# Last pair of an attention and soft-MoE kernel: 1 / sum applied behind the product with v, logits in three steps, 22 dummy transposes

## The chip, the cores and the metric

One core of a Trainium2 chip runs the whole kernel. The metric is the device time of one execution in microseconds (us); several executions are timed and their median is given. A profile of one more execution gives the span of its instructions, every instruction's start and duration, and the clock that was granted to TensorE.

The engines are PE (TensorE matmuls; PEld its weight loads), DVE (VectorE), ACT (ScalarE), POOL (GpSimd) and SP (SyncE, which issues all DMAs here). Each engine runs its instructions in the order of its queue; only semaphores tie the queues together.

## The reference

Batch 8, 8 heads, 576 tokens, head width 64, all in f32. With `tau` 0.02:

```python
scores = (q @ k.T) / 8
scores = where(scores >= max(scores, -1) - tau, scores, -1e9)
attn   = exp(scores - max(scores, -1))
attn   = attn / (sum(attn, -1) + 1e-9)
x      = concat over heads (attn @ v)             # 4608 tokens x 512
logits = x @ phi                                  # 32 slots, 4 for each of 8 experts
d = softmax(logits over all 4608 tokens);  slot_in = d.T @ x
slot_out[e] = relu(slot_in[e] @ w1[e]) @ w2[e]    # 512 -> 1024 -> 512
out = softmax(logits over the slots) @ slot_out
```

A softmax over all tokens stands between attention and the experts: no expert can start before the last token's logits are there.

## The kernel before, in words

**Attention.** The 64 (batch, head) problems are worked as 32 pairs of heads, four pairs to a batch. A pair has 576 queries x 2 heads, cut into nine chunks `i` of 128 rows: chunks 0 to 7 are four token blocks `c` for each head `h`, chunk 8 holds the 64 left-over tokens of both heads. For each chunk PE multiplies q and k (L554, L559), DVE copies the scores out negated with their row maximum (L566, "mx"), ACT takes the exponential (L576, "ex"), POOL makes the threshold (L579, "thr"), and DVE zeroes what lies under it and sums the rest (L582, "st"; the sum goes to `r[:, i]`). The probabilities lie in `p2` (one tile for each `c`) and `pL` (chunk 8). PE transposes them in 64x64 blocks (helper `ptr`, L481), ACT copies the transposes to `pTa` (c = 0, 1), `pTb` (c = 2, 3 and the left-over) and `pTl` (helper `act_copy`, L486, and L654), and PE multiplies with v in two products (L669): *a* of 256 tokens from `pTa`, *b* of 320 tokens from `pTb`. The result, features x tokens, is copied to `xT[j]`; it is transposed again (L481) into `x`, tokens x features.

**Where 1 / sum goes in.** In 31 pairs POOL scales `x` by 1 / sum behind the product (L684), and PE and ACT transpose that back into `xT` (L689, L692); only chunk 8 is scaled ahead (L613). In the last pair (`late`) the probabilities themselves are scaled as soon as a block's sums are there: two small DVE instructions make 1 / sum (L589, L591), and each chunk is multiplied with it (L595; POOL does seven chunks, DVE chunk 6; L600: ACT chunk 7). Then come the transposes.

**Dispatch.** Behind the four pairs of a batch, `dispatch(b)` transposes the left-over tokens of the four `xT` (`xl`), multiplies the four `xT` with phi (`logits`, L747, one group of 64 matmul records), takes the running maximum (L752, L755), its exponentials (L757, L759), and adds the batch's weighted tokens to `acc` (L794, L799, L807). In the last batch `scale` and `slot_in` (L719) turn `acc` into `siT`, the transposed slot inputs (L722, into the room of `phi_sb`).

**Experts.** 64 weight tiles of 512 KB are read (`load_unit`, L461 for w1, L463 for w2): 26 ahead of time into `w` tiles, 20 into `host` tiles that are laid over the attention's buffers as these come free (the pool of a `host` tile waits for the last use of the buffers below it), and 18 into `w` tiles behind the first layer's use of them. SP issues them in that order. `stage1` (L971) is the first layer, `stage2` (L1005) the second; the last quarter of stage2 writes `h00e` and `h11e`. `combine` writes the output.

**Order.** The attention part is not in program order. Each operation has a duration estimate and a rank (`nom`, from `TABLE`, added to the pair's base); a list planner (`Order.plan`) steps through time, and on each engine takes the ready operation of lowest rank for which buffers are free. So a rank decides only between operations that are ready together. PSUM has four regions, which QK scores, transposes and products share.

**Dummy transposes.** WARM transposes of the identity (L473, tile `ps`) depend on the last pair's last PE operation alone and have the highest rank: PE runs one whenever nothing else is ready, and what is left over is run at the end, ahead of stage1, in PE's queue.

Of the kernel before, what the change touches and what calls it, by code (L numbers as in the profile page):

```python
# [12 lines left out]
AF = mybir.ActivationFunctionType  # L13
ALU = mybir.AluOpType
# [16 lines left out]
REGIONS = 4  # L31
NPRE = 26
UP = 22
WARM = 38
LATE_DVE = (6,)
LATE_ACT = (7,)
FILL = 14
NHOST = 20
TABLE = {}
for _n, _v in (  # L40
# [8 lines left out]
    ]),  # L49
    ("last", [  # L50
# [7 lines left out]
    ]),  # L58
    ("end", [
        635.02, 222.30, 635.03, 884.35, 786.79, 194.11, 221.66, 209.51, 492.40, 213.82, 653.01, 233.76, 801.84, 524.02,  # L60
        811.00, 884.36, 248.25, 903.87, 542.06, 811.02, 658.66, 811.01, 811.01, 227.55, 666.83, 796.50, 632.21, 881.94,
        491.74, 653.02, 786.80,
    ]),
    ("soft", [
        27.63, 27.62, -312.54, 26.80, 28.26, -7.62,
    ]),
    ("batch", [
        -62.11, -152.03, -63.33, -1010.94, -1010.93, -130.22, -93.56, -111.14, -36.34, -160.31, -58.44, -111.55, -1032.75, -27.29,
# [6 lines left out]
        1608.61, 22.81, -920.27,  # L75
    ]),
    ("new2", [
        1255.54, -750.92, -123.71,
    ]),
    ("new3", [  # L80
        1682.14, -780.86, -618.82,
    ]),
# [39 lines left out]
           ae=0.5, x=6.0, xe=6.3, D=1.0)  # L122
# [218 lines left out]
def softmax_attention_soft_moe(  # L341
# [143 lines left out]
    def act_copy(n, nom, r, w, io):  # L485
        G.add("ACT", 51 + 0.833 * n, nom, lambda: nc.scalar.copy(*io()), r, w)  # L486

    def copy(on_dve, n, nom, r, w, io):
        if on_dve:
            G.add("DVE", 69 + 1.04 * n, nom, lambda: nc.vector.tensor_copy(*io()), r, w)  # L490
        else:
            act_copy(n, nom, r, w, io)

    def dve(dur, nom, r, w, fn):
        G.add("DVE", dur, nom, fn, r, w)

    batch = {}

    def batch_state(b):
# [6 lines left out]
    def pair(p):  # L506
# [10 lines left out]
        def pool(dur, nom, fn, r, w):  # L517
            G.add("POOL", dur, nom, fn, r, w)
# [27 lines left out]
        for i in range(N9):  # L546
# [37 lines left out]
                    scalar=thr.t, in1=view().rearrange("p (a k) -> p a k", a=2),  # L584
                    op0=ALU.is_le, op1=ALU.mult, accum_out=r.t[:, i:i + 1]))

            if late and (i == 8 or h == 1):
                e = slice(i // 2 * 2, i + 1)
                dve(68, t + OFF['ri'], [r[k] for k in range(i // 2 * 2, i + 1)], [ri[c]], lambda e=e: nc.vector.tensor_scalar(  # L589
                    out=ri.t[:, e], in0=r.t[:, e], scalar1=1e-9, scalar2=None, op0=ALU.add))  # L590
                dve(75, t + OFF['ri'], [], [ri[c]], lambda e=e: nc.vector.reciprocal(ri.t[:, e], ri.t[:, e]))  # L591
                for k in range(i // 2 * 2, i + 1):
                    dst_, view_ = (pL, lambda: pL.t) if i == 8 else (
                        p2s[c][k % 2], lambda c=c, k=k: p2s[c].t[:, k % 2 * S:(k % 2 + 1) * S])
                    f = lambda e, k=k, view=view_: e.tensor_scalar(  # L595
                        out=view(), in0=view(), scalar1=ri.t[:, k:k + 1], **one)
                    if k in LATE_DVE:
                        dve(740, t + OFF['sc'], [ri[c]], [dst_], lambda f=f: f(nc.vector))
                    elif k in LATE_ACT:
                        G.add("ACT", 650, t + OFF['sc'], lambda k=k, view=view_: nc.scalar.activation(  # L600
                            view(), view(), AF.Copy, scale=ri.t[:, k:k + 1]), [ri[c]], [dst_])
                    else:
                        pool(725, t + OFF['sc'], lambda f=f: f(nc.gpsimd), [ri[c]], [dst_])
            elif i == 8:
                e = slice(i // 2 * 2, i + 1)
                pool(292, t + OFF['ri'], lambda e=e: nc.gpsimd.tensor_scalar(
                    out=ri.t[:, e], in0=r.t[:, e], scalar1=1e-9, scalar2=1.0, op0=ALU.add, op1=ALU.mult),
                    [r[k] for k in range(e.start, e.stop)], [ri[c]])
                dve(84, t + OFF['ri'], [], [ri[c]], lambda e=e: nc.vector.reciprocal(ri.t[:, e], ri.t[:, e]))
                for k in range(e.start, e.stop):  # L610
                    dst_, view_ = (pL, lambda: pL.t) if i == 8 else (
                        p2s[c][k % 2], lambda c=c, k=k: p2s[c].t[:, k % 2 * S:(k % 2 + 1) * S])
                    pool(725, t + OFF['sc'], lambda k=k, view=view_: nc.gpsimd.tensor_scalar(  # L613
                        out=view(), in0=view(), scalar1=ri.t[:, k:k + 1], **one), [ri[c]], [dst_])
            elif not late and h == 1:
                if i == 7:
                    pool(292, t + OFF['ri'], lambda: nc.gpsimd.tensor_scalar(
                        out=ri.t[:, 0:8], in0=r.t[:, 0:8], scalar1=1e-9, scalar2=1.0, op0=ALU.add, op1=ALU.mult),
                        [r[k] for k in range(8)], [ri[0]])
                    dve(84, t + OFF['ri'], [], [ri[0]], lambda: nc.vector.reciprocal(ri.t[:, 0:8], ri.t[:, 0:8]))  # L620
                    G.skip(2)
                else:
                    G.skip(4)
# [19 lines left out]
            if i == 8:  # L643


                w = Buf("s")
                ptr(7, t + OFF['tt'], [p2s[2], p2s[3], pL], [w, pTb["t", 8], pTl["t", 8]], lambda w=w: [
                    (w.t, k * 64, [pL.t[rows[g], g * SL + k * 128:][:, 0:128] for g in range(2)]) for k in range(4)] + [
                    (w.t, 256, [pL.t[rows[0], S - 128:S], pL.t[rows[1], 0:128]])] + left_keys(2, 320, w))
                act_copy(256, t + OFF['te'], [w], [pTl[2]], lambda w=w: left_out(2, 320, w))  # L650
                act_copy(512, t + OFF['te'], [w], [pTb["L"]], lambda w=w: (
                    pTb.t[:, :, :, SM - QA:S - QA], w.t[:, :, 0:256].rearrange("p g (k q) -> p g k q", k=4)))
                for g in range(2):
                    G.add("ACT", 225, t + OFF['te'], lambda w=w, g=g: nc.scalar.copy(  # L654
                        pTl.t[rows[g], SM:S], w.t[rows[1 - g], g, 256:320]), [w], [pTl["L", g]])


        u = t0 + N9
        for a, (pT, q) in enumerate(((pTa, slice(0, QA)), (pTb, slice(QA, S)))):
            n0 = u + OFF['a1' if a else 'a0']  # L660
            w = bank_of(p == NP - 1)
            n = q.stop - q.start
            rl = [pTl[0]] if a == 0 else [pTl[2], pTl["L", 0], pTl["L", 1]]

            def mm(w=w, n=n, q=q, pT=pT):
                for kb in range(5):
                    for h in range(2):
                        v0, p0 = ((h * 4 + kb) * 64, pT.t[:, h, kb, :]) if kb < 4 else (SM + h * 64, pTl.t[:, q])
                        nc.tensor.matmul(  # L669
                            lone(w)[h * 64:(h + 1) * 64, 0:n], vv.t[:, v0:v0 + 64], p0,  # L670
                            start=(kb == 0), stop=(kb == 4), tile_position=(0, h * 64), skip_group_check=True)
            G.add("PE", 5 * (4 + 1.669 * n), n0, mm, [pT, vv] + rl, [w, xT["t"]], mode=COLS)
            copy(p == NP - 1 and a, n, n0 + OFF['ae'], [w], [xT[a]], lambda w=w, q=q, n=n: (xT.t[:, q], lone(w)[:, 0:n]))

        w = Buf("s")
        ptr(4, u + OFF['x'], [xT], [w, x["t", j]], lambda w=w: [
# [49 lines left out]
    def dispatch(b):  # L726
# [13 lines left out]

        wl = bank_of(b == B - 1)

        def logits():
            for o, q in ((slice(0, 128), lambda c: slice(c * 128, c * 128 + 128)), (slice(128, 192), lambda c: slice(SM, S))):
                for k in range(HP):
                    for c in range(4):
                        nc.tensor.matmul(  # L747
                            lone(wl)[c * 32:(c + 1) * 32, o], phi_sb[:, k, :], xT[k].t[:, q(c)], start=(k == 0),
                            stop=(k == HP - 1), tile_position=(0, 32 * c), skip_group_check=True)
        G.add("PE", 1313, u + 1, logits, xT + [ph], [wl], mode=COLS4)  # L750
        new = batch_state(b + 1)["M"]
        dve(269, u + 1.3, [wl], [M["own"]] if b else [new["run"]], lambda: nc.vector.tensor_reduce(  # L752
            out=M.t[:, 0:1] if b else new.t[:, 1:2], in_=lone(wl)[:, 0:192], axis=AX.X, op=ALU.max, negate=True))
# [392 lines left out]
```

## Time and profile before

| | |
|---|---|
| median of 3 runs (lowest, highest) | 554.12 us (554.01, 554.78) |
| profiled execution: time, span | 553.97 us, 552.2 us |
| granted TensorE clock, mean over the span | 0.988 of 2.4 GHz |
| busy share of the span | PE 96%, DVE 85%, ACT 83%, POOL 45% |
| read from HBM, written | 72.42 MB, 9.44 MB |

Attention fills the span to about 478 us, the last dispatch runs to 489 us, the experts to 520 us, and the combination and the writing of the output to the end. In the rows, "idle before" is the time in which the engine stood still ahead of the group, with what ended it; `x16` counts records, of which one f32 matmul makes two and a transpose one.

### The profile page before, as it was taken

The numbers are of one execution on the slowest core, as the hardware profiler recorded it, in microseconds if no ns is written. First come the engines' busy times: TensorE is split into PE (matmuls) and PEld (weight loads), VectorE is DVE, ScalarE is ACT, GpSimd is POOL, SyncE is SP. The second block draws the span as 40 slices with busy tenths as digits, with TensorE's granted clock in tenths as the row PEclk, the third lists the DMA queues.
The fourth block names the chain that finished last, engine by engine and source line by source line (L and its number), as shares of the span: only waits on it lengthen the run. The fifth ranks groups of instructions, "written<-read, shape, count | busy, mean of one in ns | idle before, by whom it ended". The sixth has DMA issues, their size and how long they took to land.

```text
span 552.2 us, 18305 instructions
## 1 busy us (share of the span) xinstructions
PE 530.8 (96%) x7022; PEld 340.9 (62%) x7022; DVE 470.6 (85%) x1326; ACT 458.6 (83%) x790; POOL 247.5 (45%) x478
## 2 busy tenths in 40 slices
PE   8999999999999999999999999999999998899991
PEld 6666666666666666666666666666666665654570
DVE  6999998999999998999999989998999999212192
ACT  3899998999999989998999899998999898511171
POOL 2554554554554453546454545554555547021030
PEclk9999999999999999999999999999999999899996
DMA  6355555555545543333133323333333523979498
GB/s 174 73 164 168 166 165 167 166 167 166 165 121 177 175 140 118 96 89 90 40 97 92 89 65 90 89 91 90 90 91 89 129 76 115 368 311 404 166 363 321
DMA packets 31990, 83.03 MB, mean 150 GB/s; under 512 B 4640, under 2 KB 12832, under 8 KB 31904
## 3 DMA queue, kind: packets, MB, share of 16 engines
q1 hardware_dynamic: 31904, 81.87, 48.4%
q8 instruction: 55, 0.90, 0.7%
q14 instruction: 31, 0.25, 0.2%
HBM read 72.42 MB, written 9.44 MB: 148 GB/s over the span
## 4 chain that ended last, share of the span: by engine, by line
PE 88%; DVE 4%; ACT 3%; issue 2%; POOL 1%; DVEq 0%; POOLq 0%; ACTq 0%
PE ps L669 29%; PE ps L554 24%; PE ps L481 17%; PE ps L559 3%; PE h L971 3%; PE so L1005 2%; PE ps L689 2%; PE ps L747 2%; PE ps L473 2%; PE ps L794 1%; DVE p L582 1%; PE up L421 1%; ACT pTa L486 1%; DVE ss L566 1%; DVE host L1057 1%
## 5 line engine op out<-in xcount | busy, mean ns | idle before, releaser
L566 DVE TENSOR_SCALAR_CACHE_REDUCE ss<-ps 128x576 f32<-128x576 f32 x288 | 208.9, 752 | 13.2 <-ACT pTl L486 4.9
L579 POOL TENSOR_SCALAR thr<-nmx,pabs 128x1 f32<-128x1 f32 x288 | 132.0, 460 | 179.2 <-DVE ss L566 159.6
L582 DVE SCALAR_TENSOR_TENSOR p<-ss,thr,p 128x576 f32<-128x576 f32 x256 | 202.7, 826 | 3.4 <-ACT p L576 3.1
L576 ACT ACTIVATE p<-ss,nmx 128x576 f32<-128x576 f32 x256 | 188.0, 778 | 18.8 <-DVE ss L566 18.7
L554 PE MATMUL ps<-k,q 64*128 64x288 f32 x1024 | 166.8, 427 | 0.9 <-ACT pTb L486 0.4
L481 PE MATMUL ps<-ident,p 64*128 64x64 f32 x2304 | 99.0, 225 | 3.5 <-ACT pTa L486 2.1
L481 PEld LDWEIGHTS ps<-ident,p 64*128 64x128 f32 x2304 | 88.4, 139 | 20.7 <-ACT pTa L486 3.8
L554 PEld LDWEIGHTS ps<-k,q 64*128 64x128 f32 x1024 | 83.3, 188 | 21.8 <-ACT pTl L654 5.8
L486 ACT COPY pTb<-ps 128x1024 f32<-128x1024 f32 (+1 forms) x96 | 83.7, 873 | 5.1 <-PE ps L481 2.9
L669 PE MATMUL ps<-pTb,vv 128*64 128x320 f32 x512 | 75.9, 438 | 0.0
L486 ACT COPY pTa<-ps 128x1024 f32<-128x1024 f32 x64 | 64.9, 1017 | 0.4 <-PE ps L481 0.4
L669 PE MATMUL ps<-pTa,vv 128*64 128x256 f32 x512 | 62.9, 388 | 0.0
L669 PEld LDWEIGHTS ps<-pTb,vv 128*64 128x64 f32 x512 | 33.9, 136 | 36.3 <-issue 8.5
L669 PEld LDWEIGHTS ps<-pTa,vv 128*64 128x64 f32 x512 | 34.2, 138 | 26.6 <-DVE ss L566 8.5
L669 PE MATMUL ps<-pTl,vv 128*64 128x256 f32 (+1 forms) x256 | 41.9, 406 | 0.0
L684 POOL TENSOR_TENSOR x<-x,ri 128x512 f32<-128x512 f32 x31 | 32.8, 1058 | 4.8 <-ACT x L486 4.8
L486 ACT COPY xT<-ps 128x256 f32<-128x256 f32 (+1 forms) x63 | 25.0, 397 | 7.0 <-PE ps L669 6.0
L936 POOL TENSOR_TENSOR c<-lall,crow 128x512 f32<-128x512 f32 x9 | 9.3, 1043 | 38.6 <-PE ct L473 38.6
L582 DVE SCALAR_TENSOR_TENSOR pL<-ss,thr,pL 128x576 f32<-128x576 f32 x32 | 26.5, 827 | 0.0
L669 PEld LDWEIGHTS ps<-pTl,vv 128*64 128x64 f32 x256 | 18.4, 137 | 12.7
L576 ACT ACTIVATE pL<-ss,nmx 128x576 f32<-128x576 f32 x32 | 24.8, 775 | 0.4 <-DVE ss L566 0.4
L534 POOL TENSOR_SCALAR k<-k,flag 128x576 f32<-128x576 f32 x31 | 24.0, 775 | 1.3 <-DMA k<-in_kT 1.0
(136 smaller groups left out, 553.3 us busy)
## 6 DMA issues: line engine op xcount, KB each, us to landing
w<-in_w SPq DMA_DIRECT2D x44, 512.0 KB, 7.1
q<-in_qT SPq DMA_DIRECT2D x62, 288.0 KB, 4.5
vv<-in_vt SPq DMA_DIRECT2D x32, 320.0 KB, 4.7
host<-in_w SPq DMA_DIRECT2D x20, 512.0 KB, 7.4
k<-in_kT SPq DMA_DIRECT2D x62, 144.0 KB, 3.0
out<-w SPq DMA_DIRECT2D x8, 512.0 KB, 3.3
out<-host SPq DMA_DIRECT2D x8, 512.0 KB, 5.0
out<-host SPq DMA_DIRECT2D x4, 256.0 KB, 4.5
```

The lines of the kernel that those rows point to most:

```text
L481: nc.tensor.transpose(out=s[:, g, c:c + 64], in_=ins[g], identity=ident[rows[g], rows[g]], tile_position=(64 * g, 0))
L486: G.add("ACT", 51 + 0.833 * n, nom, lambda: nc.scalar.copy(*io()), r, w)
L534: sc = lambda e, kc=kc: lambda: e.tensor_scalar(out=kt.t[:, kc], in0=kt.t[:, kc], scalar1=flag8, **one)
L554: nc.tensor.matmul(s.t[:, g, 0:HS], qt.t[rows[g], h, c * 128:(c + 1) * 128], kt.t[rows[g], h * HS:(h + 1) * HS], start=True, stop=True, ti ...
L559: nc.tensor.matmul(s.t[rows[a], g, 0:HS], qt.t[rows[g], a, SM:S], kt.t[rows[g], a * HS:(a + 1) * HS], start=True, stop=True, tile_position ...
L566: dve(674, t + OFF['mx'], [s], [ss, nmx], lambda s=s, ss=ss, nmx=nmx: nc.vector.tensor_scalar(out=ss.t.rearrange("p (a k) -> p a k", a=2), ...
L576: G.add("ACT", 668, t + OFF['ex'], lambda sv=sv, nmx=nmx, view=view: nc.scalar.activation(view().rearrange("p (a k) -> p a k", a=2), sv(), ...
L579: pool(250, t + OFF['th'], lambda nmx=nmx, thr=thr: nc.gpsimd.tensor_scalar(out=thr.t, in0=nmx.t, scalar1=1.0, scalar2=pabs, op0=ALU.mult, ...
L582: fn=lambda sv=sv, thr=thr, view=view, i=i: nc.vector.scalar_tensor_tensor(out=view().rearrange("p (a k) -> p a k", a=2), in0=sv(), scalar ...
L669: nc.tensor.matmul(lone(w)[h * 64:(h + 1) * 64, 0:n], vv.t[:, v0:v0 + 64], p0, start=(kb == 0), stop=(kb == 4), tile_position=(0, h * 64), ...
L684: G.add("POOL", 1040, u + 6.8, own=f"new{j}", r=[ri[0]], w=[x[j]], fn=lambda: nc.gpsimd.tensor_tensor(out=wide(), in0=wide(), in1=ri.t[:, ...
L971: nc.tensor.matmul(hp[n][g * 32:(g + 1) * 32, :], siT[:, kb, :], t[g][:, n * 512:(n + 1) * 512], start=(kb == 0), stop=(kb == 3), tile_pos ...
```

## The change

In the last pair the scaling of the probabilities is gone, with LATE_DVE and LATE_ACT. When all nine sums are there, DVE makes 1 / sum of all of them in two instructions, spreads it over 512 columns (`E`), PE transposes it (5 blocks of 2), ACT copies 512 and DVE 2 x 64 columns to `R`, which has the layout of `xT`. `E` and `R` take two of the four `ss` buffers. Both copies from PSUM to `xT` (before: ACT for product a, DVE for b) become a multiplication with `R` on DVE. The two 64x64 copies into `pTl` go from ACT to DVE.

The last batch's logits are three operations: pairs 0 and 1, pair 2, pair 3. In all batches the accumulation's `start` is set in the first column group alone. WARM is 22, from 38. The ranks of the last pair, of the last dispatch, of the early combination softmax (`soft`) and of the scaling behind the third and fourth pair of a batch (`new2`, `new3`) are others.

```diff
-WARM = 38
-LATE_DVE = (6,)
-LATE_ACT = (7,)
+WARM = 22
...
     ("new2", [
-        1255.54, -750.92, -123.71,
+        1064.50, -919.33, -23.80,
     ]),
     ("new3", [
-        1682.14, -780.86, -618.82,
+        2153.07, -1099.00, -31.67,
     ]),
...
-            if late and (i == 8 or h == 1):
-                e = slice(i // 2 * 2, i + 1)
-                dve(68, t + OFF['ri'], [r[k] for k in range(i // 2 * 2, i + 1)], [ri[c]], lambda e=e: nc.vector.tensor_scalar(
...
-                    if k in LATE_DVE:
-                        dve(740, t + OFF['sc'], [ri[c]], [dst_], lambda f=f: f(nc.vector))
-                    elif k in LATE_ACT:
-                        G.add("ACT", 650, t + OFF['sc'], lambda k=k, view=view_: nc.scalar.activation(
-                            view(), view(), AF.Copy, scale=ri.t[:, k:k + 1]), [ri[c]], [dst_])
-                    else:
-                        pool(725, t + OFF['sc'], lambda f=f: f(nc.gpsimd), [ri[c]], [dst_])
+            if late and i == 8:
+                dve(70, t + OFF['ri'], [r], [ri], lambda: nc.vector.tensor_scalar(
+                    out=ri.t, in0=r.t, scalar1=1e-9, scalar2=None, op0=ALU.add))
+                dve(85, t + OFF['ri'], [], [ri], lambda: nc.vector.reciprocal(ri.t, ri.t))
+                R, E, w = Buf("ss"), Buf("ss"), Buf("s")
+                dve(600, t + OFF['ri'], [ri], [E], lambda: nc.vector.tensor_copy(
+                    E.t[:, 0:SM].rearrange("p (i d) -> p i d", i=8), ri.t[:, 0:8].unsqueeze(2).to_broadcast([128, 8, 64])))
+                ptr(5, t + OFF['ri'] + .1, [ri, E], [w, R["t"]], lambda w=w: [
+                    (w.t, c * 64, [E.t[a, c * 128:(c + 1) * 128] for a in rows])
+                    for c in range(4)] + [(w.t, 256, [ri.t[a, 8:9].to_broadcast([64, 128]) for a in rows])])
+                act_copy(512, t + OFF['ri'] + .2, [w], [R["m"]], lambda w=w: (
+                    R.t[:, 0:SM].rearrange("p (c g q) -> p g c q", c=4, g=2),
+                    w.t[:, :, 0:256].rearrange("p g (c q) -> p g c q", c=4)))
+                for g in range(2):
+                    dve(136, t + OFF['ri'] + .2, [w], [R["L", g]], lambda w=w, g=g: nc.vector.tensor_copy(
+                        R.t[rows[g], SM:S], w.t[rows[g], g, 256:320]))
+                spreads.append(R)
...
-            copy(p == NP - 1 and a, n, n0 + OFF['ae'], [w], [xT[a]], lambda w=w, q=q, n=n: (xT.t[:, q], lone(w)[:, 0:n]))
+            if late:
+                dve(69 + 1.04 * n, n0 + OFF['ae'], [w, spreads[0]], [xT[a]], lambda w=w, q=q, n=n: nc.vector.tensor_tensor(
+                    out=xT.t[:, q], in0=lone(w)[:, 0:n], in1=spreads[0].t[:, q], op=ALU.mult))
+            else:
+                act_copy(n, n0 + OFF['ae'], [w], [xT[a]], lambda w=w, q=q, n=n: (xT.t[:, q], lone(w)[:, 0:n]))
...
-        def logits():
+        def logits(ks):
...
-                            lone(wl)[c * 32:(c + 1) * 32, o], phi_sb[:, k, :], xT[k].t[:, q(c)], start=(k == 0),
+                            lone(wl)[c * 32:(c + 1) * 32, o], phi_sb[:, k, :], xT[k].t[:, q(c)], start=(k == 0 and not o.start),
...
-        G.add("PE", 1313, u + 1, logits, xT + [ph], [wl], mode=COLS4)
+        for ks in ((range(HP),) if b < B - 1 else (range(2), range(2, 3), range(3, HP))):
+            G.add("PE", 1313 * len(ks) / HP, u + 1, lambda ks=ks: logits(ks), [xT[k] for k in ks] + [ph], [wl], mode=COLS4)
```

In the new ranks of the last dispatch the third logits step has 207.07 on base 288; the last pair's transposes of `xT` have 314.22 on base 279 and those into `xl` 485.77 on base 288; the first two logits steps have 499.92 and 473.76 on base 288; the products 328.07 and 339.72 on base 279.

## Rows read from the trace of the kernel before

**Rows 1.** Chain of waits, 440 to 492 us: start, length (us), what held it.
```profile
455.06 2.31 PE ps L669 x20
...
459.75 2.87 PE ps L669 x20
...
464.68 1.16 PE ps L481 x32
...
465.90 0.77 ACT pL L576
...
466.78 0.82 DVE p L582 x3
467.60 1.22 DVE pL L582 x2
468.81 0.97 DVE ri L589 x2
...
470.54 1.86 PE ps L481 x30
472.41 5.64 PE ps L669 x40
...
478.13 0.50 DVE xT L490
...
478.77 0.71 PE ps L481 x16
479.49 1.46 PE ps L747 x64
480.94 0.91 PE ps L473 x7
...
486.94 2.12 PE ps L473 x19
...
489.11 3.19 PE h L971 x25
```

**Rows 2.** PE in order of time, 465 to 471 us: start, length, what; idle before.
```profile
467.61 0.28 PE L481 MATMUL ps<-ident,p 64*128 64x64 f32 x2 [1.79 <-ACT pTa L486]
468.25 0.77 PE L481 MATMUL ps<-ident,p 64*128 64x64 f32 x18 [0.36 <-POOL p L595]
469.76 0.46 PE L689 MATMUL ps<-ident,x 64*128 64x64 f32 x8 [0.74 <-POOL x L684]
470.54 1.12 PE L481 MATMUL ps<-ident,p 64*128 64x64 f32 x16 [0.32 <-DVE p L595]
```

**Rows 3.** Stretches: length, busy of PE, PEld, DVE, ACT, POOL; clock, DMA share, GB/s.
```profile
470.00:475.00 5.00, 4.68 (x58) 3.43 (x56) 0.49 (x1) 4.22 (x8) 0.99 (x1) 0.66 0.96 325
...
480.00:485.00 5.00, 5.00 (x119) 3.78 (x109) 2.95 (x13) 2.37 (x8) 0.00 (x0) 1.00 1.02 408
...
489.00:490.00 1.00, 0.94 (x11) 0.29 (x14) 0.00 (x0) 0.00 (x0) 0.00 (x0) 1.00 0.64 246
...
516.00:517.00 1.00, 1.00 (x16) 0.34 (x12) 0.00 (x0) 0.00 (x0) 0.00 (x0) 1.00 0.38 139
```

**Rows 4.** Groups of the page: busy us, mean ns; idle before and what ended it.
```profile
L582 DVE SCALAR_TENSOR_TENSOR p<-ss,thr,p 128x576 f32<-128x576 f32 x256 | 202.7, 826 | 3.4 <-ACT p L576 3.1
...
L486 ACT COPY pTa<-ps 128x1024 f32<-128x1024 f32 x64 | 64.9, 1017 | 0.4 <-PE ps L481 0.4
...
L684 POOL TENSOR_TENSOR x<-x,ri 128x512 f32<-128x512 f32 x31 | 32.8, 1058 | 4.8 <-ACT x L486 4.8
```

**Rows 5.** ACT in order of time, a copy of 512 columns.
```profile
471.54 0.59 ACT L692 COPY xT<-ps 128x512 f32<-128x512 f32 x1
```

**Rows 6.** DVE in order of time: the copy into siT, and a pass with two operands.
```profile
486.98 0.29 DVE L722 COPY phi_sb<-ps 128x128 f32<-128x128 f32 x1 [1.23 <-PE ps L719]
...
519.80 0.42 DVE L1031 TENSOR_TENSOR so_sb<-h00e,so_sb 128x256 f32<-128x256 f32 x1 [8.79 <-ACT so_sb L1093]
```

**Rows 7.** PE in order of time, the last quarter of stage2.
```profile
518.63 1.05 PE L1005 MATMUL h00e<-w,hz 128*32 128x256 f32 x16
```

More of the change, by code (lines that the diff above doesn't have):

```diff
@@ L50 @@
     ("last", [
[7 rows of a table removed]
[6 rows of a table added]
     ]),
     ("end", [
-        635.02, 222.30, 635.03, 884.35, 786.79, 194.11, 221.66, 209.51, 492.40, 213.82, 653.01, 233.76, 801.84, 524.02,
-        811.00, 884.36, 248.25, 903.87, 542.06, 811.02, 658.66, 811.01, 811.01, 227.55, 666.83, 796.50, 632.21, 881.94,
-        491.74, 653.02, 786.80,
+        485.77, -220.65, 499.92, 473.76, 207.07, 696.27, 668.17, -167.25, -240.09, -248.45, 503.04, -243.91, 516.89, -175.94,
+        721.61, 456.32, 689.18, 680.56, -185.26, 672.03, 466.78, 728.43, 486.12, 696.85, 668.74, -238.85, 474.31, 718.85,
+        493.29, 678.16, 466.77, 511.30, 698.57,
     ]),
     ("soft", [
-        27.63, 27.62, -312.54, 26.80, 28.26, -7.62,
+        239.33, 245.74, -551.88, 251.93, 248.34, 244.23,
     ]),
@@ L495, in dve @@
         G.add("DVE", dur, nom, fn, r, w)
+    spreads = []
     batch = {}
@@ L585, in pair @@
                     op0=ALU.is_le, op1=ALU.mult, accum_out=r.t[:, i:i + 1]))
-            if late and (i == 8 or h == 1):
-                e = slice(i // 2 * 2, i + 1)
-                dve(68, t + OFF['ri'], [r[k] for k in range(i // 2 * 2, i + 1)], [ri[c]], lambda e=e: nc.vector.tensor_scalar(
[L590 to L596, printed above, removed]
-                    if k in LATE_DVE:
-                        dve(740, t + OFF['sc'], [ri[c]], [dst_], lambda f=f: f(nc.vector))
-                    elif k in LATE_ACT:
-                        G.add("ACT", 650, t + OFF['sc'], lambda k=k, view=view_: nc.scalar.activation(
-                            view(), view(), AF.Copy, scale=ri.t[:, k:k + 1]), [ri[c]], [dst_])
-                    else:
-                        pool(725, t + OFF['sc'], lambda f=f: f(nc.gpsimd), [ri[c]], [dst_])
@@ L653, in pair @@
                 for g in range(2):
-                    G.add("ACT", 225, t + OFF['te'], lambda w=w, g=g: nc.scalar.copy(
-                        pTl.t[rows[g], SM:S], w.t[rows[1 - g], g, 256:320]), [w], [pTl["L", g]])
+                    f = lambda e, w=w, g=g: e(pTl.t[rows[g], SM:S], w.t[rows[1 - g], g, 256:320])
+                    if late:
+                        dve(136, t + OFF['te'], [w], [pTl["L", g]], lambda f=f: f(nc.vector.tensor_copy))
+                    else:
+                        G.add("ACT", 225, t + OFF['te'], lambda f=f: f(nc.scalar.copy), [w], [pTl["L", g]])
         u = t0 + N9
@@ L672, in pair @@
             G.add("PE", 5 * (4 + 1.669 * n), n0, mm, [pT, vv] + rl, [w, xT["t"]], mode=COLS)
-            copy(p == NP - 1 and a, n, n0 + OFF['ae'], [w], [xT[a]], lambda w=w, q=q, n=n: (xT.t[:, q], lone(w)[:, 0:n]))
+            if late:
+                dve(69 + 1.04 * n, n0 + OFF['ae'], [w, spreads[0]], [xT[a]], lambda w=w, q=q, n=n: nc.vector.tensor_tensor(
+                    out=xT.t[:, q], in0=lone(w)[:, 0:n], in1=spreads[0].t[:, q], op=ALU.mult))
+            else:
+                act_copy(n, n0 + OFF['ae'], [w], [xT[a]], lambda w=w, q=q, n=n: (xT.t[:, q], lone(w)[:, 0:n]))
         w = Buf("s")
@@ L741, in dispatch @@
         wl = bank_of(b == B - 1)
-        def logits():
+        def logits(ks):
             for o, q in ((slice(0, 128), lambda c: slice(c * 128, c * 128 + 128)), (slice(128, 192), lambda c: slice(SM, S))):
-                for k in range(HP):
+                for k in ks:
                     for c in range(4):
                         nc.tensor.matmul(
-                            lone(wl)[c * 32:(c + 1) * 32, o], phi_sb[:, k, :], xT[k].t[:, q(c)], start=(k == 0),
+                            lone(wl)[c * 32:(c + 1) * 32, o], phi_sb[:, k, :], xT[k].t[:, q(c)], start=(k == 0 and not o.start),
                             stop=(k == HP - 1), tile_position=(0, 32 * c), skip_group_check=True)
-        G.add("PE", 1313, u + 1, logits, xT + [ph], [wl], mode=COLS4)
+        for ks in ((range(HP),) if b < B - 1 else (range(2), range(2, 3), range(3, HP))):
+            G.add("PE", 1313 * len(ks) / HP, u + 1, lambda ks=ks: logits(ks), [xT[k] for k in ks] + [ph], [wl], mode=COLS4)
         new = batch_state(b + 1)["M"]
```

13 rows, old and new, of the table TABLE are left out of this document.

## The prediction

> **What bounds the kernel now.** I read the page first: PE is busy 96% of the span, so a gain must come from time in which PE stands still, repeats itself or runs at the low clock. Then the windows, in which PE is poor only around the end of the last pair. So I read the chain of waits there, then PE's own timeline, then the DMA share of the stages behind it.
>
> The chain [rows 1] shows how the last pair ends. The last exponential ends at 466.67, two st follow on DVE, then 0.97 us for the last 1 / sum, 0.76 to the first transposes of the last scaled block, 1.86 of transposes, and only then the two products from 472.41 to 478.05. Behind them come the copy (0.50), the transposes of `xT` (0.71), the logits (1.46, done at 480.95), and some 6 us of dispatch to 486.94. Then PE runs 19 dummy transposes (2.12 us), and stage1 starts at 489.11.
>
> PE's rows in this stretch [rows 2] show 1.79 + 0.36 + 0.74 + 0.32 = 3.21 us of idling, each ended by something that waits for scaled probabilities, by a copy queued behind it, or by the POOL's other work. The stretch behind it [rows 3] has a mean granted clock of 0.66: part of it ran at 1.2 instead of 2.4 GHz. The price can be read off: 30 transpose records took 1.86 us where 32 took 1.16 just before [rows 1], 0.77 too much; the two products took 5.64 where the pair before took 2.31 + 2.87 = 5.18 [rows 1], 0.46 too much. Together 1.23 us.
>
> **Part 1, the scaling leaves the path.** Up to 464.68 PE does the same with and without the change, and the chain lies on it there, so I count PE's work from there to the end of product b: 478.05 - 464.68 = 13.37 us before. Gone are the waits for scaling; if all idling goes, 3.21, and with it the low clock, 1.23. Added are 10 transposes for `R`, one record each: 10 x 1.16 / 32 = 0.36 [rows 1], so 0.4. That leaves 9.3 us, so product b would end at 474.0.
>
> Does another engine forbid it? DVE: without the L589 and L591 groups between its st, and without POOL beside it, the last st cost what they cost on average: the mean of L582 is 826 ns [rows 4], and pL's took 1.22 [rows 1]. Behind the exponential's end at 466.67, two st end near 468.4 instead of 468.82. `pL`'s transposes need 0.5 us and ACT's copies of them about 1 us, so product b may start from 470; in PE's count it starts at 474.0 - 2.87 = 471.1. ACT: from 464 it has three exponentials (0.77 each [rows 1]), four copies of 1024 (1.02 each [rows 4]) and small ones; it loses the scaling of chunk 7 and gains one copy of 512, 0.59 as its nearest row has it [rows 5]. 2.3 + 4.1 + 0.6 is 7 us, so until 471: as late as PE, and so some idling will stay.
>
> `E` does not appear in the trace. From below I take DVE's copy of 320 columns, 0.50 us [rows 1]; from above a full st, 0.83 [rows 4]; nearest is the first, with 512 columns some 0.7. With 1 / sum that makes 468.4 + 0.3 + 0.7 = 469.4, transposes 469.8, ACT's copy 470.4 or a copy later. `R` is needed when product a is done, 471.1: hidden, with 0.7 us to spare. If ACT takes it late, product a's multiplication waits, which costs nothing as long as it ends ahead of b's. The multiplications replace copies: 0.42 for 256 columns with a second operand [rows 6] against 0.50 for 320 without [rows 1], so for 320 near 0.5; from both sides between 0.0 and 0.1 more. I take 0. Moving the 64x64 copies from ACT to DVE helps the engine that is full and costs the one that is then idle: 0.
>
> **Part 2, the logits in three steps.** 64 records took 1.46 us, so three quarters are 1.10 and the last pair's step 0.37. The last step has a lower rank than the transposes of `xT` and so runs ahead of them; these 0.71 us move into the wait for the maximum, where 7 dummies (0.91 us) stood [rows 1]. The path behind product b is then 0.72 (to the end of the multiplication and PE's start, as from 478.05 to 478.77) + 0.37. The 1.10 of the first two steps is PE work all the same. If PE idles before, they are free; if PE is full, they lengthen it: 474.0 + 1.1 + 0.72 + 0.37 = 476.2, or 475.5 if part of them fills the 0.72. If half of the idling stays (1.6), they fit into it: 474.0 + 1.6 + 0.72 + 0.37 = 476.7. Without either, 475.1 would be the end. I take 476.0 for the end of the logits: 4.9 us earlier than 480.95. Bounds: 475.1 (5.8), and 478.2 (2.7) if all of the idling stays but the low clock goes.
>
> **Part 3, the dispatch behind the logits.** Its chain of small steps, 480.95 to 486.94, stays. New beside it are ACT's copies of `x` and `xl`, which before ran under the logits and now stand where ACT is wanted for the exponentials: between 0 and one copy, 0.59 [rows 5]. I take 0.1, as only one of the two can be in the way at a time and ACT has idle time there.
>
> **Part 4, 16 dummies fewer.** 19 of the 38 stood in waits, 19 at the end: 2.12 / 19 = 0.112 us each. What stage1 really waits for is the copy of `siT`, which ends at 487.27 [rows 6]; 489.11 is 1.7 us behind that with some 0.15 for the semaphore. After the change the first wait takes transposes of `xT` instead of 7 dummies, the others still some 12, so of 22 about 8 to 10 are left. With 8: 11 fewer at the end, 1.2 us. Bounds: 10 left (1.0), or so few that the copy decides (1.7).
>
> **Part 5, the weights.** A stage1 that starts 6 us earlier asks for its weights earlier. Reads run at 408 GB/s [rows 3], 524,288 bytes in 1.28 us. The 20 `host` loads end within 489 to 490, the last of 18 `w` loads within 516 to 517 [rows 3], and the last quarter of stage2, which needs it, starts at 518.63 [rows 7]. So the last weights have 2 us of cover as it is. But the 18 wait today for stage1 to free the slots: if they follow the `host` loads without a gap, the last lands at 489.6 + 18 x 1.28 = 512.6, and the quarter could start 6.0 us earlier. The `host` loads themselves move too, since they wait for `p2`, `pTa` and `pTb`: up to 3 us earlier where DMA is not full. So DMA is just hidden. Behind stage2 all moves along.
>
> **Part 6, the steady part.** New ranks for the scaling behind the third and fourth pairs decide only where operations are ready together. On PE and ACT these ranks lie, before and after, under those of all that can be ready beside them; on POOL, 45% busy, the third pair's moves past few. I take 0, between -0.5 and +0.5.
>
> **Sum.** 4.9 - 0.1 + 1.2 = 6.0 us, just what the weights allow. The profiled execution took 553.97 us for a span of 552.2, so 548.0; the median of the runs lies 0.15 above that execution. I say 547.9.
>
> **Rivals.**
> 1. *The low clock stays.* Before, the clock fell behind a stretch in which PE had only transposes and idling [rows 2, 3]. Afterwards the stretch ahead of product a still has transposes alone, denser, with the early logits. If it falls again, the 1.23 us of the rows come back: 549.2. For it: nothing but idling went. Against it: the 19 dummies and what surrounds them ran at full clock, as 480 to 485 us shows [rows 3]. The Trainium skill, "TensorE: Matmul & The Clock Gate", section "Part 4: PE-mode transpose", speaks for it: transposes do not count as work for the clock as products do ("it doesn't count as PE-busy the same way"). By that rule the denser transposes would not help, and this rival would be the forecast; the trace has a full clock over a stretch of many transposes, yet not without products, so it leaves the rule open. Chance 0.13.
> 2. *The weights end the gain.* `R` lives in an `ss` buffer until the last multiplication, and a `host` tile lies over it. If `host` loads end one or two loads later than now, the last weights land at 513.9 or 515.2 and the quarter starts there: a gain of 4.7 or 3.4, 549.3 to 550.6. For it: DMA's share is 0.96 in 470 to 475 already [rows 3]. Against it: all other buffers come free earlier. Chance 0.12.
> 3. *The scaling was not what it waited for*: ACT's copies set the pace, all idling stays, only the clock, the logits' last quarter and the dummies pay: 2.7 + 1.0 = 3.7, with part 3's copy in the way 3.1: 550.3 to 550.9. Chance 0.06.
> 4. *More than forecast*: PE runs through, the steps fill the waits, the copy of `siT` decides: 5.8 + 1.7 and earlier `host` loads, 546.4 or below. Chance 0.08.
> 5. *Slower.* POOL's scaling `x` behind the third pair of each batch now goes ahead of a threshold for which DVE waits. One takes 1.06 us [rows 4]; seven batches, 7.4 us: 547.9 + 7.4 = 555.3. It decides from 0.86 us in each batch on. For it: DVE is near full in the steady part. Against it: POOL idles more than half, so the two are seldom ready at once. Chance 0.04; a smaller share of it that just eats the gain up, 0.02.
>
> **How the numbers follow.** The forecast, 546.6 to 549.0, has 0.55. The range 545.8 to 550.6 takes in rivals 1 and 2 and most of 4. A difference under 0.2% (1.1 us) cannot be told from none here. Faster: all but rival 5, 0.94; within 0.2%: 0.02; slower: 0.04.
>
> **What would show it.** Right: product b ends near 474 in place of 478, no L595 on POOL, 16 logits records right behind the multiplication, 8 or so dummies ahead of stage1, stage1 near 483, its matmuls and stage2's without idling, granted clock 1.0 throughout 465 to 480. Wrong: PE idling of 2 us or more behind 465 (rival 3), a clock of 0.5 in product a (1), PE waiting for DMA in stage1 or in `h00e` (2), a stage1 that moved otherwise than the whole, or a last pair that starts later than 452 (5).

## The result, and the profile after

The changed kernel took 549.59 us (median of 5, 548.74 to 549.63) against 554.33 (median of 5, 554.01 to 555.0): ratio 0.9908, interval 0.9893 to 0.9922, 4.7 us faster; forecast were 6.0 and 547.9. The profiled execution took 549.61 us, 4.36 less than that of before, over a span of 547.8. In the experiments the same kernel took 548.62 against 555.01 for before (ratio 0.9892, 0.9877 to 0.9907, which is 6.0 us, as forecast). The two intervals overlap; what the profiles show of the difference is told below.

In the rows of after the lines have moved: L478 and L483 are the helpers of transposes and ACT's copies, L580 the st, L564 the mx, L670 the products, L652 the 64x64 copies into `pTl`, L675 the multiplication with `R`, L752 the logits, L470 the dummies, L977 and L1011 stage1 and stage2.

The chain of waits of after, as in [rows 1]:

```profile
455.22 2.31 PE ps L670 x20
...
463.45 1.86 PE ps L478 x58
465.31 0.54 PE ps L552 x4
465.86 0.65 PE ps L557 x8
...
466.97 2.31 PE ps L670 x20
...
469.96 0.55 ACT pTb L483
...
471.77 0.23 DVE pTl L652
...
472.37 2.93 PE ps L670 x20
...
475.87 0.55 PE ps L752 x10
...
476.83 0.59 ACT x L483
...
477.99 0.58 ACT xl L483
...
482.93 1.12 PE ps L470 x10
484.05 6.13 PE h L977 x53
```

Nothing of 1 / sum is on it any more, product a (466.97) runs 5.4 us earlier and apart from b, and two rows stand there that before had none: ACT's copies of `x` and `xl`, inside the dispatch. All of it starts 0.16 us later than before (455.22 against 455.06); that is less than the profiled executions below differ from each other in this place (0.8 us).

| | before | after | earlier by | forecast |
|---|---|---|---|---|
| product b ends | 478.05 | 475.30 | 2.75 | 4.0 |
| logits end | 480.95 | 476.42 | 4.53 | 4.9 |
| `slot_in` ends (dispatch: 5.99, 6.51) | 486.94 | 482.93 | 4.01 | 4.8 |
| stage1 starts | 489.11 | 484.05 | 5.06 | 6.0 |
| last quarter of stage2 starts | 518.63 | 513.99 | 4.64 | 6.0 |

DVE in order of time, then two stretches with the columns of [rows 3]:

```profile
465.98 0.76 DVE L564 TENSOR_SCALAR_CACHE_REDUCE ss<-ps 128x576 f32<-128x576 f32 x1 [1.71 <-ACT pTa L483]
...
470.14 0.43 DVE L590 COPY ss<-ri 128x512 f32<-128x512 f32 x1
...
472.68 0.46 DVE L599 COPY ss<-ps 64x64 f32<-64x64 f32 x2 [0.45 <-ACT ss L483]
473.17 0.42 DVE L675 TENSOR_TENSOR xT<-ps,ss 128x256 f32<-128x256 f32 x1
475.32 0.49 DVE L675 TENSOR_TENSOR xT<-ps,ss 128x320 f32<-128x320 f32 x1 [1.73 <-PE ps L670]
```

```profile
470.00:475.00 5.00, 4.65 (x92) 3.33 (x88) 1.84 (x7) 2.32 (x4) 0.00 (x0) 1.00 0.97 347
...
513.00:514.00 1.00, 1.00 (x13) 0.26 (x8) 0.00 (x0) 0.00 (x0) 0.00 (x0) 1.00 0.08 33
```

The granted clock is 1.00 where before it was 0.66 [rows 3]. `E` took 0.43 us, less than either bound; `R` was complete at 473.14 and product a's multiplication waited for it, but product b's came 1.7 us later, so it stayed hidden. The last packets of weights move within 513 to 514, where the last quarter of stage2 starts. That is the new wait; the weight loads' waits of after say so, and before had none for DMA in this stretch (columns: us in total, times, longest):

```profile
PEld h L977 <- DMA host<-in_w: 0.4, 1, 0.4
PEld so L1011 <- DMA w<-in_w: 0.3, 1, 0.3
PEld h00e L1011 <- DMA w<-in_w: 0.2, 1, 0.2
```

A weight load runs ahead of its matmul (in before from 518.20 for the quarter's first at 518.63), so not every such wait costs time: a_ref below has the second and the third of these and lost nothing. Sharper is when the last read of 512 KB lands. SP's rows of it, before (issued at 508.0) and after (504.1), each with its time from issue to landing:

```profile
L463 SPq DMA_DIRECT2D w<-in_w x1: 328/328/328, 508.0 to 508.0; - x1
DMA to landing us min/median/max: 10.1/10.1/10.1
```

```profile
L460 SPq DMA_DIRECT2D w<-in_w x1: 328/328/328, 504.1 to 504.1; - x1
DMA to landing us min/median/max: 10.1/10.1/10.1
```

Before, it landed at 518.1, 0.5 us ahead of the quarter's start at 518.63 [rows 7]; after, at 514.2, 0.2 us behind the start at 513.99.

### The profile page after: what moved, and what is told of

Read it like the earlier page. It is cut to its first block, busy times and chain, and to the rows that moved or that the text cites. A ratio compares the mean times of both kernels' runs of the same rounds, so it can differ in the third digit from the quotient of the medians.

```text
span 547.8 us, 18279 instructions
## 1 busy us (share of the span) xinstructions
PE 530.0 (97%) x7016; PEld 339.4 (62%) x7016; DVE 469.6 (86%) x1323; ACT 457.5 (84%) x787; POOL 240.8 (44%) x471
## 4 chain that ended last, share of the span: by engine, by line
PE 87%; DVE 5%; ACT 4%; issue 2%; DVEq 0%; POOL 0%; POOLq 0%; ACTq 0%
PE ps L670 29%; PE ps L552 24%; PE ps L478 17%; PE ps L557 3%; PE h L977 3%; PE so L1011 2%; PE ps L694 2%; PE ps L752 2%; PE ps L800 1%; DVE p L580 1%; PE ps L470 1%; PE up L418 1%; DVE cT L969 1%; ACT pTa L483 1%; DVE ss L564 1%
## 5 line engine op out<-in xcount | busy, mean ns | idle before, releaser
L564 DVE TENSOR_SCALAR_CACHE_REDUCE ss<-ps 128x576 f32<-128x576 f32 x288 | 209.0, 752 | 15.7 <-ACT pTl L483 4.9
L580 DVE SCALAR_TENSOR_TENSOR p<-ss,thr,p 128x576 f32<-128x576 f32 x256 | 201.8, 824 | 3.5 <-ACT p L574 3.1
L478 PE MATMUL ps<-ident,p 64*128 64x64 f32 x2304 | 98.0, 223 | 0.9 <-ACT pTa L483 0.3
L478 PEld LDWEIGHTS ps<-ident,p 64*128 64x128 f32 x2304 | 87.6, 138 | 18.0 <-issue 2.8
L483 ACT COPY pTb<-ps 128x1024 f32<-128x1024 f32 (+1 forms) x96 | 84.0, 876 | 5.5 <-PE ps L478 3.3
L670 PE MATMUL ps<-pTb,vv 128*64 128x320 f32 x512 | 76.0, 439 | 0.4 <-DVE pTl L652 0.4
L483 ACT COPY pTa<-ps 128x1024 f32<-128x1024 f32 x64 | 64.9, 1018 | 0.4 <-PE ps L478 0.4
L670 PE MATMUL ps<-pTa,vv 128*64 128x256 f32 x512 | 62.3, 385 | 0.0
L670 PEld LDWEIGHTS ps<-pTb,vv 128*64 128x64 f32 x512 | 34.1, 136 | 36.4 <-issue 8.9
L670 PEld LDWEIGHTS ps<-pTa,vv 128*64 128x64 f32 x512 | 33.9, 136 | 26.2 <-DVE ss L564 8.5
L670 PE MATMUL ps<-pTl,vv 128*64 128x256 f32 (+1 forms) x256 | 41.9, 406 | 0.0
L483 ACT COPY xT<-ps 128x256 f32<-128x256 f32 (+1 forms) x62 | 24.6, 398 | 6.2 <-PE ps L670 5.1
L670 PEld LDWEIGHTS ps<-pTl,vv 128*64 128x64 f32 x256 | 18.4, 137 | 12.6
L580 DVE SCALAR_TENSOR_TENSOR pL<-ss,thr,pL 128x576 f32<-128x576 f32 x32 | 26.0, 813 | 0.0
L483 ACT COPY pTl<-ps 128x256 f32<-128x256 f32 x64 | 24.2, 378 | 0.4 <-PE ps L478 0.4
(140 smaller groups left out, 546.6 us busy)
```

The source lines that it names most:

```text
L478: nc.tensor.transpose(out=s[:, g, c:c + 64], in_=ins[g], identity=ident[rows[g], rows[g]], tile_position=(64 * g, 0))
L564: dve(674, t + OFF['mx'], [s], [ss, nmx], lambda s=s, ss=ss, nmx=nmx: nc.vector.tensor_scalar(out=ss.t.rearrange("p (a k) -> p a k", a=2), ...
L580: fn=lambda sv=sv, thr=thr, view=view, i=i: nc.vector.scalar_tensor_tensor(out=view().rearrange("p (a k) -> p a k", a=2), in0=sv(), scalar ...
L670: nc.tensor.matmul(lone(w)[h * 64:(h + 1) * 64, 0:n], vv.t[:, v0:v0 + 64], p0, start=(kb == 0), stop=(kb == 4), tile_position=(0, h * 64), ...
```

## The experiments

Twelve kernels, four or five executions each (b_logits3_warm22 twelve), on three chips, each time beside the kernel before: a_ref to a_nox_warm12 on one (before took 555.01 there), a_logits1 to a_warm38 on the next (554.63), a_warm0 to b_logits3_warm22 on the third (554.83). So medians of different groups are from different chips; the changed kernel itself ran in the first group only. The last pair starts up to 0.8 us earlier or later from one profiled execution to the next, so the stages are counted from product b of the third-last pair (447.17 to 447.93; 447.44 in before, 447.59 in after), as PE's order of time shows it. "Expert stages" is from stage1's start to the first product of the combination; 31.36 us is its length when it waits for no weights.

| kernel | median us (lowest to highest) | logits end | dispatch | stage1 starts | expert stages | their end |
|---|---|---|---|---|---|---|
| before (profile of the result) | 555.01, 554.63, 554.83 | 33.51 | 5.99 | 41.67 | 31.36 | 73.03 |
| after (the result; before: 554.33) | 549.59 | 28.80 | 6.54 | 36.39 | 32.15 | 68.54 |
| a_ref: the changed kernel | 548.62 (548.47-548.85) | 28.80 | 6.54 | 36.39 | 31.36 | 67.75 |
| a_warm12 | 548.66 (548.06-549.97) | 28.80 | 6.53 | 35.71 | 32.39 | 68.10 |
| a_nox | 548.78 (548.46-549.27) | 28.80 | 6.53 | 36.38 | 31.36 | 67.74 |
| a_nox_warm12 | 548.08 (547.96-548.24) | 28.79 | 6.53 | 35.70 | 31.37 | 67.07 |
| a_logits1 | 549.73 (549.63-550.10) | 29.81 | 6.52 | 37.38 | 31.36 | 68.74 |
| a_qkfirst | 550.22 (550.07-550.44) | 30.13 | 6.53 | 37.72 | 31.36 | 69.08 |
| a_disp | 548.68 (548.59-549.51) | 28.80 | 6.55 | 36.08 | 31.76 | 67.84 |
| a_warm38 | 551.04 (550.45-551.65) | 28.79 | 6.53 | 38.12 | 31.36 | 69.48 |
| a_warm0 | 549.07 (548.34-549.79) | 28.80 | 6.48 | 35.67 | 31.80 | 67.47 |
| a_disp_warm0 | 548.81 (548.12-548.98) | 28.81 | 5.64 | 34.83 | 33.09 | 67.92 |
| b_warm22 | 552.33 (552.28-553.33) | 33.54 | 6.00 | 40.02 | 31.36 | 71.38 |
| b_logits3_warm22 | 554.96 (553.96-556.16) | 34.86 | 6.53 | 42.45 | 31.36 | 73.81 |

**Do the weights hold the end?** Four kernels. a_ref is unchanged.

> The changed kernel itself, as the measure for the other runs on this chip. Theory W (the weights' reads now hold the tail back by 0.7 us or more: stage1 waits for a host tile, the last quarter of stage2 for the last tile) and rival P (PE's own path through the last pair, the dispatch and the dummies decides alone) both expect 549.6 us and a gain over before of 4.4 to 4.8 us.

> The changed kernel with 12 dummy transposes instead of 22: the 10 that stand ahead of stage1 go (1.1 us), of which about 0.75 us were on PE's path (the copy of siT ends 0.3 us behind the last product). W: stage1 starts 0.75 us earlier and waits that much longer for its weights, time 0.0 to 0.3 us below the changed kernel. P: 0.75 us below it.

```diff
-WARM = 22
+WARM = 12
```

> The changed kernel without the reads of six w1 tiles (units 12 to 17; stage1 uses six other tiles in their place, so this part of the product is not the reference's). DMA has 7.7 us less to do. W: both waits for weights go and the time falls by 0.7 us. P: no change, within 0.2 us.

```diff
         i, kind, _, e, k = units[len(where)]
-        where[i] = t
+        where[i] = where[i + 14] if i in X else t
+        if i in X:
+            return
```

> Six reads left out as in a_nox (their part of the product is not the reference's), and 12 dummies. W: now the dummies count, 0.7 + 0.75 = 1.4 to 1.5 us below the changed kernel. P: 0.75 us below it, as with all reads.

a_ref lost nothing to weights: its expert stages took 31.36, as in before, where after took 32.15, and its time is 548.62 and not the 549.6 that both theories expected. After lost its 0.79 us in two places: when stage1's first transposes into `ht` begin it is 0.49 us behind a_ref, and the other 0.30 fall in the last quarter of stage2. Both executions issued the last `host` read some 10 us ahead of its landing; it landed at 491.3 in after and at 490.4 in a_ref, and stage1 waited for it in after alone. From 470 to 474 DMA moved 313 to 344 GB/s in after and 375 to 389 in a_ref; why, is open. So theory W is wrong for a_nox (nothing to win back: 67.74 against 67.75) and right for a_warm12: stage1 started 0.68 us earlier, and the expert stages took 1.03 longer. Its weight loads waited:

```profile
PEld so L1011 <- DMA w<-in_w: 0.6, 2, 0.3
...
PEld h00e L1011 <- DMA w<-in_w: 0.4, 1, 0.4
...
PEld h L977 <- DMA host<-in_w: 0.3, 1, 0.3
```

With six reads fewer (a_nox_warm12 has both edits) the same 12 dummies do pay: 67.07, 0.67 less than a_nox, and 0.7 in the medians; none of its weight loads waited for DMA. That is P's 0.75 and not the 1.4 to 1.5 that W added up. So the changed kernel's stage1 starts where the reads are just in time: in a_ref the last one lands at 513.3 for a quarter that starts at 513.47. A little to either side decides whether an execution loses 0.8 us (after's) or none.

**What are the 16 dummies worth?**

> The changed kernel with 38 dummies again: 26 instead of 10 ahead of stage1, 16 x 0.112 = 1.8 us. Theory E (weights hold stage1 and stage2 only from the changed kernel's start of stage1 on, not behind it): no waits for weights are left, time 1.3 to 1.8 us above the changed kernel. Rival W (weights had the lead by 0.7 us or more already): 1.1 us or less above it.

> The kernel before with 22 dummies instead of 38 and nothing else. 19 stand in waits, so 3 are left ahead of stage1, less than the copy of siT takes. Theory E (the dummies ahead of stage1 cost what lies beyond that copy, and the weights of before have 2 us of cover): stage1 1.5 to 1.75 us earlier, time 1.5 to 1.75 us below before. Rival H (what stands behind them hides it: the clock falls, or weights hold): less than 0.8 us.

(The edit is WARM alone, to 38 and to 22.) In both, stage1 moves by 1.65 to 1.73 us and the expert stages stay at 31.36: theory E's path, rivals W and H out. In the times it is more than E and the path give: 2.4 for a_warm38 (medians of two chips; the medians of the spans, 548.6 and 546.8, differ by 1.8) and 2.5 for b_warm22. The ratio of b_warm22, 0.9959 (0.9947 to 0.9971), is 1.6 to 2.9 us, so no more is claimed.

**Three steps or one.**

> The changed kernel with the last batch's logits as one operation again, behind the last pair's multiplication. Theory S (the first 48 records fill a wait: product b waits for the copies into pTl until 472.4 in any case): product b starts as before, PE idles about 1.4 us ahead of it, the logits end 1.1 us later, and the time is 0.9 to 1.2 us above the changed kernel. Rival F (PE is full there, the steps only move work): product b starts 1.1 us earlier and the time stays within 0.2 us.

```diff
-        for ks in ((range(HP),) if b < B - 1 else (range(2), range(2, 3), range(3, HP))):
+        if b == B - 1:
+            G.skip(2)
+        for ks in (range(HP),):
```

PE in order of time of a_logits1:

```profile
472.29 2.37 PE L670 MATMUL ps<-pTb,vv 128*64 128x320 f32 x16 [1.15 <-DVE pTl L652]
474.46 0.74 PE L670 MATMUL ps<-pTl,vv 128*64 128x320 f32 x4
475.79 1.53 PE L752 MATMUL ps<-xT,phi_sb 128*32 128x128 f32 x64 [0.58 <-DVE xT L675]
```

Product b starts where it did, PE idles 1.15 us ahead of it, and the logits end 1.0 us later (1.1 us between the medians, of two chips). Theory S: in the changed kernel the first 48 records fill a wait for the copies into `pTl`. It is these copies, then, that set product b's start, with the steps and without.

**The same steps without the new way of scaling.**

> The kernel before with the three logits steps, the new ranks of the last dispatch and 22 dummies, but with the last pair's scaling as before. Theory S: product b ends where it did (478.0 +- 0.4), the logits end 1.1 us behind it instead of 2.9, the dispatch takes 6.5 us instead of 6.0, 10 dummies instead of 19 stand ahead of stage1: 1.8 - 0.5 + 1.0 = 2.3 us below before; so the scaling alone is worth the rest to the changed kernel, 2.7 to 3.7 us. Rival R (the steps help only without the scaling, as PE's idling ahead of the products is not long enough for them): 1.2 us or less below before.

The edit puts the three steps, the new ("end", ...) ranks and this into the kernel before:

```diff
-WARM = 38
+WARM = 22
```

Theory S fails here; rival R has the number, but not the reason. PE in order of time:

```profile
464.86 0.87 PE L747 MATMUL ps<-xT,phi_sb 128*32 128x128 f32 x32
...
471.95 3.39 PE L669 MATMUL ps<-pTa,vv 128*64 128x256 f32 x16 [0.44 <-ACT pTa L486]
475.11 0.90 PE L669 MATMUL ps<-pTl,vv 128*64 128x256 f32 x4
...
476.41 0.53 PE L481 MATMUL ps<-ident,pL 64*128 64x64 f32 x10
...
478.45 2.37 PE L669 MATMUL ps<-pTb,vv 128*64 128x320 f32 x16 [1.39 <-ACT pTl L654]
```

The steps themselves found idle time, but from 464.86 on the logits hold one of the four PSUM regions. The planner now puts `pL`'s transposes behind product a (476.41, before 471.45), product b waits for their copies and starts at 478.45 instead of 475.16, and product a runs at the low clock (granted 0.50 from 473 to 475; 4.06 us to its end against 2.31 [rows 1], and 2.99 in before's own last pair). What the fewer dummies gave is lost again: ratio 1.0001 (0.9992 to 1.001). The region as the reason is read from the order, not tried alone. So the parts don't add up, and this run gives no price for the scaling by itself.

**Was it the late st that kept product b from 474.0?** In after, PE ran 48 transposes ahead of the last two QK, DVE stood still 1.71 us, and the last st ended 0.8 us later than before (469.6 against 468.8), not 0.4 earlier.

> The changed kernel with the last pair's QK of chunks 4 and 8 ranked ahead of its transposes; nothing else. In the changed kernel PE runs 48 transposes ahead of these two QK, DVE stands still 1.7 us and ends its last st at 469.6 instead of 468.8. Theory Q (PE's total decides, not DVE's end): the last st ends 1 to 1.7 us earlier, product a moves behind the transposes, product b ends at 475.3 +- 0.5 all the same and the time stays within 0.4 us. Rival D (the late st are why product b missed 474.0): product b ends 0.8 to 1.3 us earlier, and the time falls by 0.3 to 1.0 us as far as the weights allow.

```diff
-        -325.80, 279.35, -299.08, 348.39, 60.24, -281.30, 140.44, 82.97, 324.26, 119.35, -281.71, 128.54, 60.25, 313.06,
+        -325.80, 279.35, -299.08, 300.00, 60.24, -281.30, 140.44, 82.97, 324.26, 119.35, -281.71, 128.54, 60.25, 313.06,
...
-        -159.00, 295.45, 59.11, -316.84, 149.02, 92.59, 309.38, 32.16, -284.55, 171.11, 80.93, 345.40, -153.91, 365.51,
+        -159.00, 295.45, 59.11, -316.84, 149.02, 92.59, 309.38, 32.16, -284.55, 171.11, 80.93, 345.40, -153.91, 301.00,
```

Both theories miss: the last st ended 0.8 us earlier, and product b 1.3 us later. PE in order of time:

```profile
469.14 1.21 PE L478 MATMUL ps<-ident,p 64*128 64x64 f32 x32 [1.14 <-ACT pTa L483]
...
471.88 1.95 PE L670 MATMUL ps<-pTa,vv 128*64 128x256 f32 x16 [0.17 <-ACT pTb L483]
...
474.08 2.32 PE L670 MATMUL ps<-pTb,vv 128*64 128x320 f32 x16
```

Transposes that come later hand ACT its copies later; PE waits for ACT at 469.14, and product a, which in after ran at 466.9 while ACT copied, is now on the path. DVE's idling was the price of giving ACT its work early, and a good one: the logits end 1.3 us later without it.

**Why did the dispatch grow from 6.0 to 6.5 us?**

> The changed kernel with ACT's copy of x put behind the exponential of the logits and the copy of xl on DVE; otherwise the same. Theory C (these two copies lengthened the dispatch from 6.0 to 6.5 us): from the logits' end to slot_in's end 5.8 to 6.1 us, stage1 0.5 us earlier; the weights then take back most of it, so the time is 0 to 0.4 us below the changed kernel. Rival N (the chain of maximum, exponential and transposes sets this length by itself): 6.4 to 6.6 us as before, no change.

```diff
+        if late:
+            put_off.append(lambda w=w: G.add("ACT", 477, (NP - 1) * N9, xcopy, [w], [x[j]], after=[len(G.ops) - 1], own="put_off"))
...
-        act_copy(512, u + .3, [w], [xl[0]], lambda w=w: (
+        copy(b == B - 1, 512, u + .3, [w], [xl[0]], lambda w=w: (
...
+        if b == B - 1:
+            put_off[0]()          # right behind the exponential dT; the rank of xl is 674.00
```

6.55, as the rival said. But in a_disp the exponential dT started at 476.92, 0.07 behind the maximum's end, and PE's order of time shows who was late instead:

```profile
476.84 0.88 PE L470 MATMUL ps<-ident 128*128 128x128 f32 x6
477.64 0.27 PE L478 MATMUL ps<-ident,M 64*128 64x64 f32 x2
477.85 0.33 PE L470 MATMUL ps<-ident 128*128 128x128 f32 x1
478.10 0.34 PE L478 MATMUL ps<-ident,dT 64*128 64x64 f32 x4
```

Dummies stand in PE's queue ahead of the transposes of the maximum and of dT, as many as the planner's estimates called for, and hold them. Hence the last pair of runs:

> The changed kernel without any dummies. Theory G (dummies queued ahead of the transposes of the maximum and of dT hold the dispatch, but ACT's copies of x and xl hold it as well): dispatch 6.2 to 6.6 us as with them, stage1 0.75 us earlier, time within 0.4 us of the changed kernel as the weights hold. Rival K (the dummies keep the clock up): the granted clock falls behind 478 and the time rises by 0.5 us or more.

> No dummies, and the copies of x and xl out of the exponential's way as in a_disp. Theory G (either of the two alone holds the dispatch, which is why a_disp still took 6.55 us): now the dispatch takes 5.7 to 6.0 us and stage1 starts 1.2 to 1.5 us earlier than in the changed kernel; the weights take most of that back, time 0 to 0.5 us below it. Rival N (the length is that of the chain itself): 6.4 us or more. Rival K as in a_warm0.

(WARM = 0 in the changed kernel and in a_disp.) Dispatch: 6.54 with both, 6.55 and 6.48 with one of the two, 5.64 with neither. Theory G: either alone is enough to hold it (5.64 is a little under the 5.7 to 6.0 that it gave). Rival K falls: in a_disp_warm0 the granted clock is 1.00 in each 5 us from 460 to 495, without any dummy. The time is again the weights' affair: stage1 starts 1.56 us earlier than in a_ref, and the expert stages take 33.09. Its weight loads' waits:

```profile
PEld h L984 <- DMA host<-in_w: 1.9, 3, 1.1
...
PEld so L1018 <- DMA w<-in_w: 0.6, 2, 0.3
...
PEld h00e L1018 <- DMA w<-in_w: 0.2, 1, 0.2
```

No version with all reads beat the changed kernel by more than the noise (ratios 0.9889 to 0.9899, a_ref 0.9892): whatever starts stage1 earlier, at 34.83 to 36.39, has its expert stages end at 67.5 to 68.5.

## Why the prediction was right, and where its sum was off

The mechanism and most terms held; 549.59 lies in the wide range, above the narrow one (546.6 to 549.0). The forecast should also have read 554.12 - 6.0 = 548.1: the 0.15 between median and profiled execution went in with the wrong sign.

1. *Scaling off the path, product b at 474.0.* It ended at 475.30. PE's waits for scaled probabilities went, and the low clock with them: of 3.21 us of idling 0.35 is left ahead of b, and the 1.23 stands. But b does not start when PE is free, as the count from PE alone has it. It waits for ACT's copies into `pTb` and DVE's two into `pTl`, which end at 472.24, where the prediction let these copies release b from 470. a_logits1 shows it: without the 48 records PE idles, and b starts no earlier. That PE's count with the steps, 464.68 + 9.3 + 1.1 = 475.1, comes so near to 475.30 is chance: the steps just fit into the wait. Product a went ahead of `pL`'s transposes, and the last st ended later, not earlier; a_qkfirst shows that this was no loss.
2. *Logits' end, 476.0.* 476.42, of which 0.15 came with the start. The steps' worth is shown by a_logits1 (1.0 us on the path), for this order only.
3. *Dispatch, 0.1 longer.* This term was mis-sized: 0.52, near the upper bound of 0.59. The prediction named ACT's copies; it did not see that dummies sized for the planner's estimates hold the path as well. The 2 x 2 of dummies and copies shows both.
4. *16 dummies, 1.2 us.* 10 were left over, not 8, and stage1 followed 0.8 us behind the copy of `siT` (483.25) instead of 1.84: 1.04, the lower bound. All 16 are worth 1.65 to 1.73 on PE's path.
5. *Weights just hidden, 0.* In a_ref yes (31.36), in after's profiled execution not quite (32.15, 0.79 longer). That is rival 2 in part, by a smaller amount than its first price of 1.3. The 2 us of cover [rows 3, 7] were a misreading: the fall of DMA's share at 516 to 517 says that most of the reading is done, and not that the tile has landed (518.1). By the landings the cover was 0.5 us, and the `host` reads of before ended at 491.5, not 489.6. That the 18 reads behind them would follow without a gap was right (491.3 + 18 x 1.28 = 514.3, and the last landed at 514.2). So the reads came 3.9 us earlier (4.8 in a_ref), which with 0.5 of cover allows 4.4 us (5.3), and not 6.0. Rival 2's own ground, a `host` tile that comes late because of `R`, did not hold after up: the last six `host` reads of after were issued at 475.4 to 481.1 and landed at 484.9 to 491.3, with DMA's share at 0.98 or more from 474 to 512, so they stood in a full queue.
6. *Steady part, 0.* The third-last pair's product b came at 447.59 against 447.44, inside what executions differ by.

The sum with measured terms: 4.53 - 0.52 + 1.05 - 0.79 = 4.3, as the profiled executions differ (4.36). Without the weights' 0.79 it is 5.1 with after's other terms, and a_ref's path gives that. Its times show 6.0 (5.2 to 6.8); where the rest comes from is not shown, as no execution of before was profiled there.

Of the rivals, the low clock did not come back (rival 1): the granted clock was 1.00 throughout 465 to 480. Whether transposes alone would have held it, no run here shows: between 463 and 476 QK, products and logits alternate with them. The Trainium skill, "TensorE: Matmul & The Clock Gate", section "Part 4: PE-mode transpose", says that full clock does not engage for transposes. Of rival 3 it is true that ACT's copies hold product b, but the idling did not stay. Rivals 4 and 5 did not happen.

## What to carry to other kernels

Ask of every gain where the next transfer lands: a_disp_warm0 started stage1 1.56 us earlier than a_ref, and all of it (end at 67.92 against 67.75) was taken back by reads. And take a transfer's end from its landing, not from where DMA's share falls: that was worth 1.5 us of cover that was not there. A filler instruction in an in-order queue is free only behind the last thing that anyone waits for; put into a wait by estimate, it holds the path when the wait ends early. And a step moved into idle time takes its buffers along: the same three logits steps won 1.0 us in one order, and in the other they lost what 16 fewer dummies had given.

## What was not expected of the hardware

A dummy alone between 64x64 transposes held PE 0.25 us (from 477.85 to 478.10 in a_disp); in a row each takes 0.112 [rows 1]. The copy of 1 / sum over 512 columns, each value 64 times, took 0.43 us on DVE, as long as a multiplication of 256 columns from PSUM (0.42). And PE kept the full clock through a dispatch without dummies in which it was busy 3.40 of 5 us (475 to 480 in a_warm0):

```profile
475.00:480.00 5.00, 3.40 (x78) 2.39 (x80) 2.44 (x11) 2.74 (x8) 0.00 (x0) 1.00 1.03 414
```
